# Matmuls on constants at the start of a recurrence kernel, and a planner that counts its first weights as landing later

## The chip, the cores and the metric

The kernel runs on one core of a Trainium2 chip. The metric is the device time of one execution in microseconds (us). The core has a matrix engine (TensorE, PE in the profile, with weight loads as PEld), a vector engine (VectorE, DVE), a scalar engine (ScalarE, ACT), GpSimd (POOL) and SyncE (SP), which issues the DMAs. Each takes its instructions in the order in which they were written, and waits on semaphores for the others.

## The reference

Two blocks. The first is a linear recurrence per batch and head, with q, k, v and a gate of shape (4, 8, 768, 48); the second multiplies two projections of its output and projects the product twice. All arithmetic that counts is float32; the four weight matrices come as float64.

```python
f = 1.0 / (1.0 + np.exp(-f_logit))
for t in range(S):
    state = f[:, :, t, :, None] * state + np.einsum('bhd,bhe->bhde', k[:, :, t], v[:, :, t])
    y[:, :, t] = np.einsum('bhd,bhde->bhe', q[:, :, t], state)
x = y.transpose(0, 2, 1, 3).reshape(B * S, H * D)      # 3072 x 384
a = x @ w1                                             # 384 -> 1024
b = x @ w2
return ((a * b) @ w3) @ w_out                          # 1024 -> 1024 -> 384
```

## The kernel before

The sequence is cut into 24 chunks of 128 steps (u = 0 to 23; six to a batch entry). For each chunk, `attention(u)` forms the running products of the gates forward (`forward`, L329) and backward (`backward`, L351) with two scans on VectorE, scales q and k by them (`scale_q` L345, `scale_k` L359), and multiplies the two on TensorE (`pairs`, L370, into the PSUM tile `pa`). ScalarE copies that out as A (`taken`, L379), GpSimd masks it to be causal (`causal`, L385), and TensorE multiplies it with v (`value`, L420) and adds what the state carries in (L428 for the first four chunks, L435 later). For the state, TensorE transposes K (`turn`, L396, into the PSUM tile `pk`), ScalarE copies it (`turned`, L404), TensorE multiplies it with v (`update`, L456, again into `pk`), and VectorE adds and scales (`state`, L466 to L472). ScalarE puts the state into blocks (`blocks`, L478). The output goes to `ys` (`outcome`, L485); of the first four chunks it is put in place by TensorE with a permutation `perm` (`moved`, L509, and `settled`, L514), later by DMAs (`gather`, L504).

Four chunks make a token block of 512. `ffn(n)` multiplies it by w1 and w2 (all through `three`, L530), forms the product a*b, and multiplies by w3 and w_out folded into one matrix `wc` (`fold`, L984). From the second block on, the products follow a scheme with seven instead of eight block products, with sums on VectorE.

The weights come in float64 and are turned to float32 on the chip. `fetch` (L871) loads a piece of 128 rows with one DMA (L897) into one of five raw buffers, which later loads use again once their last reader, L927, is done. `sub` then turns each half-piece of 512 columns with two operations on ScalarE (`magnitude` L916, `rest` L919) and on VectorE `shifted` (L922, L923), `signed` (L927) and `joined` (L933). Loads 0 to 2 are w1, loads 3 to 5 are w2, then w_out and w3 follow. The first half of the columns of w1 is due first.

No order of instructions is written by hand. Every step is a task of `Plan` (L73) with an engine, a cost in us, the tasks that it depends on and a priority, and `order` (L92) builds a schedule greedily: of all tasks it takes the one that can start earliest, by priority among those that start at the same time. The tasks are then emitted by their planned start, and this fixes the order on every engine. Loads go through `moves` (L286): a task on SP for the issue and one on a queue called DMA for the transfer, whose readers may start a `lag` of 1.3 us after it. The costs and lags are constants of the kernel and decide only the order; on the chip each instruction waits for its semaphores. SP issues the loads of the first four chunks and of five weight pieces one after the other, from 1.35 to 17.6 us.

Before the plan is emitted, `setup` (L236) clears buffers and makes constants. The one that matters here is `floor`, a tile of 112 partitions by 512 columns filled by VectorE at L248 and L249, with 2^-60 and a few ones. The PSUM tile `pk` has one buffer, used in turn by `turn`, `update` and, at the very end, `judge`.

Of the kernel before, what the change touches and what calls it, by code (L numbers as in the profile page):

```python
# [36 lines left out]
F32 = mybir.dt.float32  # L37
# [8 lines left out]
P = 128  # L46
# [3 lines left out]
HP = H // 2  # L50
R = 64 + D
# [13 lines left out]
TH = TB // 2  # L65
# [59 lines left out]
@with_exitstack  # L125
def kernel(
    ctx: ExitStack,
    tc: tile.TileContext,
    q: bass.AP,
    k: bass.AP,  # L130
    f_logit: bass.AP,
    v: bass.AP,
    w1: bass.AP,
    w2: bass.AP,
    w3: bass.AP,
    w_out: bass.AP,
    leaf_mask: bass.AP,
    out: bass.AP,
):
    nc = tc.nc  # L140
    const = ctx.enter_context(tc.tile_pool(name="const", bufs=1))
    ident = const.tile([P, P], F32, name="ident")
    w12 = const.tile([P, 2, KM, DFF], F32, name="w12")
    wc = const.tile([P, KF, DM], F32, name="wc")
    left = const.tile([1, 1], I32, name="left")
    with tc.manual_schedule():
        outside = ranged(tc, q, k, f_logit, v, w1, w2, w3, w_out, out, ident, w12, wc, left)
        with tc.If(outside > 0, preferred_fallthrough_block=True, label="general"):
            general(tc, q, k, f_logit, v, leaf_mask, out, ident, w12, wc)
# [12 lines left out]
def rows(par):  # L162
    return slice(64 * par, 64 * par + D)
# [10 lines left out]
def ranged(ctx, tc, q, k, f_logit, v, w1, w2, w3, w_out, out, ident, w12, wc, left):  # L174

    nc = tc.nc
# [10 lines left out]
    ps = ctx.enter_context(tc.tile_pool(name="ps", bufs=1, space=PSUM))  # L187
    ps_f = ctx.enter_context(tc.tile_pool(name="ps_f", bufs=NF, space=PSUM))

    floor = keep.tile([R, NQ], F32, name="floor")  # L190
# [35 lines left out]
    plan = Plan()  # L226
# [3 lines left out]
    moving = plan.add("PE", 0.0, lambda: None, takes=["ab"], prio=-1e9)  # L230
    coming = plan.add("PE", 0.0, lambda: None, takes=["ab"], prio=-1e9)

    def heads(t):
        return t.rearrange("p (h c) -> p h c", c=C)

# [44 lines left out]
    def need(u):  # L280
        return (0.0, 1.0, 2.0, 3.0)[u] if u < 4 else 45.0 + 14.5 * (u - 4)

    def past(u, n, *names):
        return [tk[u - n][nm] for nm in names if u >= n and nm in tk[u - n]]

    def moves(issue, size, rate, emit, deps, prio):  # L286

        i = plan.add("SP", issue, emit, deps, prio, lag=0.6)
        return plan.add("DMA", size / rate, lambda: None, [i], prio, lag=1.3)

    def attention(u):
        s, t = st[u], tk[u]
        opens, closes = u % NCH == 0, u % NCH == NCH - 1
        n0 = need(u)
# [38 lines left out]
        def last():  # L333
            nc.scalar.copy(lasts[:, u], heads(s["P"])[:, :, C - 1])
# [3 lines left out]
        def ends():  # L338
            nc.vector.reciprocal(heads(back)[:, :, C - 1], heads(s["P"])[:, :, C - 1])
# [109 lines left out]
        if not closes:  # L449
            def update():  # L450
                s["pd"] = ps.tile([P, HP, R], F32, name="pk")[0:R, :, 0:D]
                for hp in range(HP):
                    for par in range(2):
                        h = 2 * hp + par
                        w = 64 if par == 0 else D
                        nc.tensor.matmul(  # L456
                            s["pd"][64 * par : 64 * par + w, hp], lhsT=s["kt"][:, hp, 64 * par : 64 * par + w],
                            rhs=s["v"][:, h * D : h * D + D], start=True, stop=True,
                        )

            t["s"] = plan.add("PE", 0.6, update, [t["e"], t["lv"]] + past(u, 1, "d"), n0 - 997)

            def state():
                s["S"] = work.tile([R, HP, D], F32, name="S")
                s["G"] = work.tile([R, HP], F32, name="G")
                nc.vector.tensor_tensor(s["G"], lasts[:, u], heads(gate[(u + 1) % 2][:, 0:NQ])[:, :, 0], ALU.mult)  # L466
                gain = s["G"].unsqueeze(2).to_broadcast([R, HP, D])
                if opens:
                    nc.vector.tensor_tensor(s["S"], s["pd"], gain, ALU.mult)
                else:  # L470
                    nc.vector.tensor_tensor(s["S"], s["pd"], st[u - 1]["S"], ALU.add)
                    nc.vector.tensor_tensor(s["S"], s["S"], gain, ALU.mult)  # L472

            t["d"] = plan.add("DVE", 0.55 if opens else 0.9, state, [t["s"], t["l"]] + past(u, 2, "b"), n0)

            def blocks():
                for par in range(2):
                    nc.scalar.copy(sb[u % 2][rows(par), :, 64 * par : 64 * par + D], s["S"][rows(par)])  # L478

            t["b"] = plan.add("ACT", 0.75, blocks, [t["d"]] + past(u, 1, "v"), n0)  # L480
# [10 lines left out]
        n = u // UB  # L491
# [379 lines left out]
    def fetch(loads_, a, prio, subs, deps=()):  # L871

        total = subs[-1][1]
        if not wide:
            def plain():
                for place_, src in loads_:  # L880
                    for c0, c1, dst, _, _ in subs:
                        d = dst().rearrange("p (a m) -> p a m", a=a)
                        m = (c1 - c0) // a
                        b0 = c0 // a if len(subs) > 1 else 0
                        nc.sync.dma_start(d[place_], src[:, :, b0 : b0 + m])
            waits = [d for sub in subs for d in sub[4]]
            ld = plan.add("SP", 1.9 * total / 512, plain, waits, prio, lag=2.0)
            return [ld] * len(subs)
        load_no = len(users)
        buf = load_no if load_no < len(raws) else (load_no - len(raws)) % NRAW  # L890
        raw = raws[buf][:, 0 : 2 * total]
        words = raw.rearrange("p (n two) -> p n two", two=2)
        held = [g for no, b_, gs in users if b_ == buf for g in gs]

        def load():
            for place_, src in loads_:
                nc.sync.dma_start(raw.rearrange("p (a m) -> p a m", a=a)[place_], src.bitcast(U32))  # L897

        ld = moves(0.45, total, 380, load, held[-2:], prio)
        asked.append(ld)  # L900
        got = []
        users.append((load_no, buf, got))
        ends = []

        def sub(c0, c1, dst, due, waits):
            n = c1 - c0
            w = n / 512
            lo, hi = words[:, c0:c1, 0], words[:, c0:c1, 1]
            a0 = spot[0] if n <= 512 else (spot[0] + 512) // 1024 * 1024 % 2048
            spot[0] = (a0 + (512 if n <= 512 else 1024)) % 2048  # L910
            m = magnitudes[:, a0 : a0 + n]
            mine = range(a0 // 512, (a0 + n + 511) // 512)
            s = {}

            def magnitude():
                nc.scalar.activation(m, hi.bitcast(F32), AF.Abs)  # L916

            def rest():
                nc.scalar.activation(lo.bitcast(F32), lo, AF.Copy, bias=2.0, scale=2.0**-51)  # L919

            def shifted():
                nc.vector.tensor_scalar(m, m, HIGH, LOW, ALU.min, ALU.max)  # L922
                nc.vector.tensor_scalar(m.bitcast(U32), m.bitcast(U32), 3, None, ALU.logical_shift_left)  # L923

            def signed():
                s["to"] = dst()
                nc.vector.scalar_tensor_tensor(  # L927
                    s["to"].bitcast(U32), hi, 0x80000000, lo, ALU.bitwise_and, ALU.bitwise_or
                )

            def joined():
                to = s["to"].bitcast(I32)
                nc.vector.tensor_tensor(to, m.bitcast(I32), to, ALU.add)  # L933

            past = [joins[i] for i in mine if i in joins]
            b = plan.add("ACT", 0.2 + 0.43 * w, magnitude, [ld] + past, due)
            e = plan.add("ACT", 0.2 + 0.43 * w, rest, [ld], due)
            h = plan.add("DVE", 0.32 + 0.54 * w, shifted, [b], due)
            g = plan.add("DVE", 0.16 + 0.53 * w, signed, [e, b] + list(waits), due)
            j = plan.add("DVE", 0.16 + 0.53 * w, joined, [h, g], due - 1)  # L940
            parts.append((g, j))
            joins.update({i: j for i in mine})
            got.append(g)
            ends.append(j)

        for one_ in subs:
            sub(*one_)
        return ends
# [104 lines left out]
    for u in range(NU):  # L1053
        attention(u)
        if u == 3:
            weights()
        if u == NU - 1:
            judged = plan.add("DVE", 1.5, judge, [tk[i]["y"] for i in range(NU)], -20)
        if u % UB == UB - 1:
            ffn(u // UB)  # L1060
# [340 lines left out]
```

## Time and profile before

| | us |
|---|---|
| median of 5 runs | 507.74 |
| lowest and highest of them | 507.44, 508.65 |
| the profiled execution | 508.19 |
| its span in the profile | 505.8 |
| TensorE busy in the span | 486.8 |
| VectorE busy in the span | 363.2 |
| ScalarE busy in the span | 161.8 |

What follows was read from this one profiled execution; 2.4 us of its time lie outside the span. A line of the timeline gives the start, the length, the engine, the line of the code, the operation, what it writes and reads with the shapes, and how many instructions were merged; in brackets stand the engine's idle time before it and what ended that. A float32 matmul appears as two instructions. The start of the kernel is the part to look at: the first chunk's products begin at 8.50 us, and the first product with w1 at 36.26.

### The profile page before, as it was taken

To read this page: it belongs to the slowest core of one execution; us is meant where nothing else is said; L and a number is where in the kernel's file an instruction comes from. 1 tells how busy PE (TensorE), PEld (TensorE's weight loads), DVE (VectorE), ACT (ScalarE), POOL (GpSimd) and SP (SyncE) were. 2 spreads that over 40 slices of the span, in tenths; PEclk is the share of its full clock that TensorE was granted. 3 is DMA by queue.
4 is the path that set the end of the run, shared out by engine and by line. 5 is a ranking of instruction groups with operands and counts; after the bars stand their busy time and mean duration, and the time that the engine had idled before them with its cause. 6 is when DMAs were issued, how large, how long until landed. Compare 5 with 4: busy or idle time off the path is not lost.

```text
span 505.8 us, 8806 instructions
## 1 busy us (share of the span) xinstructions
PE 486.8 (96%) x3346; PEld 406.9 (80%) x3346; DVE 363.2 (72%) x701; ACT 161.8 (32%) x340; POOL 42.8 (8%) x51
## 2 busy tenths in 40 slices
PE   3889999999999999999999999999999999999995
PEld 2778854666698887889878899888899888889994
DVE  6899999999988769866677766256564677564541
ACT  4689464863434345212432112321010011011000
POOL 8120010010011201001110000110000000000000
PEclk9999999999999999999999999999999999999999
DMA  5978466853123265311160001210002100000011
GB/s 174 365 246 271 132 232 214 258 186 90 47 79 92 59 191 171 87 36 45 44 192 16 1 6 32 61 46 0 2 21 61 45 1 0 1 0 1 32 49 52
DMA packets 30163, 46.02 MB, mean 91 GB/s; under 512 B 6560, under 2 KB 20384, under 8 KB 28320
## 3 DMA queue, kind: packets, MB, share of 16 engines
q1 hardware_dynamic: 30112, 45.38, 28.6%
q8 instruction: 28, 0.46, 0.4%
q14 instruction: 23, 0.19, 0.1%
HBM read 36.70 MB, written 4.72 MB: 82 GB/s over the span
## 4 chain that ended last, share of the span: by engine, by line
PE 90%; DVE 4%; SPq 2%; POOL 1%; DMA 1%; issue 1%; ACT 0%; POOLq 0%; DVEq 0%; ACTq 0%
PE f L530 67%; PE f L984 8%; PE pa L370 4%; PE pa L420 4%; PE pk L456 2%; PE pa L435 2%; PE pk L396 2%; SPq L504 1%; DVE fwd L329 1%; PE f L420 1%; DMA ab<-in_f_logit_dram 1%; DMA vt<-in_v_dram 1%; DVE bwd L351 0%; DVE Q L345 0%; SPq L299 0%
## 5 line engine op out<-in xcount | busy, mean ns | idle before, releaser
L530 PE MATMUL f<-xt,w 128*128 128x256 f32 (+1 forms) x600 | 160.1, 397 | 0.0
L530 PEld LDWEIGHTS f<-xt,w 128*128 128x128 f32 x600 | 112.9, 190 | 24.4 <-issue 9.5
L530 PE MATMUL f<-place 128*128 128x192 f32 (+1 forms) x504 | 114.0, 351 | 0.0
L530 PEld LDWEIGHTS f<-place 128*128 128x128 f32 x504 | 87.3, 190 | 6.8 <-issue 1.1
L385 POOL TENSOR_SCALAR_AFFINE_SELECT A<-A 128x1024 f32<-128x1024 f32 x24 | 31.5, 1313 | 293.5 <-ACT A L379 293.5
L984 PE MATMUL f<-place 128*128 128x384 f32 x128 | 43.1, 490 | 0.0
L633 ACT COPY a<-f 128x256 f32<-128x256 f32 x36 | 13.4, 372 | 75.4 <-PE f L530 59.7
L530 PE MATMUL f<-xt,place 128*128 128x256 f32 x144 | 37.2, 381 | 0.0
L984 PEld LDWEIGHTS f<-place 128*128 128x128 f32 x128 | 23.8, 190 | 15.8 <-issue 0.7
L530 PE MATMUL f<-wc,ab 128*128 128x192 f32 x192 | 35.7, 329 | 0.0
L329 DVE TENSOR_TENSOR_SCAN fwd<-gate,floor 112x512 f32<-112x512 f32 x24 | 30.6, 1275 | 2.8 <-ACT gate L321 1.8
L530 PEld LDWEIGHTS f<-wc,ab 128*128 128x128 f32 x192 | 31.8, 190 | 0.9
L657 DVE TENSOR_TENSOR place<-f,a 128x256 f32<-128x256 f32 x36 | 15.2, 423 | 23.8 <-PE f L530 23.6
L379 ACT COPY A<-pa 128x1024 f32<-128x1024 f32 x24 | 24.2, 1010 | 22.0 <-PE pa L370 22.0
L370 PEld LDWEIGHTS pa<-Q,K 48*128 48x128 f32 x384 | 24.8, 198 | 6.9 <-issue 4.7
L351 DVE TENSOR_TENSOR_SCAN bwd<-gate,back 112x512 f32<-112x512 f32 x24 | 29.8, 1240 | 0.8
L530 PEld LDWEIGHTS f<-xt,place 128*128 128x128 f32 x144 | 26.9, 189 | 3.8 <-DVE place L657 0.2
L370 PE MATMUL pa<-Q,K 48*128 48x128 f32 x384 | 29.5, 296 | 0.0
L485 ACT ACTIVATE ys<-pa 112x512 f32<-112x512 f32 x20 | 11.9, 597 | 40.8 <-PE pa L435 21.9
L396 PE MATMUL pk<-ident,K 112*128 112x112 f32 x80 | 12.4, 280 | 11.5 <-DVE K L359 10.3
L919 ACT ACTIVATE place<-place 128x512 f32<-128x512 uint32 (+2 forms) x24 | 21.1, 890 | 7.2 <-DMA place<-in_w_out_dram 4.4
L916 ACT ACTIVATE place<-place 128x512 f32<-128x512 f32 (+2 forms) x24 | 21.2, 885 | 6.6 <-DVE w L933 4.0
(104 smaller groups left out, 624.6 us busy)
## 6 DMA issues: line engine op xcount, KB each, us to landing
place<-in_w_dram SPq DMA_DIRECT2D x14, 1024.0 KB, 5.2
vt<-in_v_dram SPq DMA_DIRECT2D x24, 192.0 KB, 2.9
out_dram<-o SPq DMA_DIRECT2D x24, 192.0 KB, 2.0
q<-in_q_dram SPq DMA_DIRECT2D x46, 96.0 KB, 2.4
f<-in_f_logit_dram SPq DMA_DIRECT2D x44, 96.0 KB, 2.7
k<-in_k_dram SPq DMA_DIRECT2D x44, 96.0 KB, 2.6
place<-in_w_out_dram SPq DMA_DIRECT2D x4, 768.0 KB, 5.3
xt<-ys SPq DMA_DIRECT2D x120, 24.0 KB, 1.8
```

Source lines behind the costliest of these rows:

```text
L329: nc.vector.tensor_tensor_scan(s["P"], gate[u % 2][:, 0:NQ], floor, 0.0, ALU.mult, ALU.max)
L351: nc.vector.tensor_tensor_scan(s["R"][:, ::-1], gate[u % 2][:, NQ:0:-1], back[:, ::-1], 0.0, ALU.mult, ALU.max)
L370: nc.tensor.matmul(s["pa"][:, par, cols], lhsT=s["K"][rows(par), cols], rhs=s["Q"][rows(par), cols], start=True, stop=True,)
L379: nc.scalar.copy(s["A"].rearrange("p r h c -> p r (h c)"), s["pa"])
L385: nc.gpsimd.affine_select(out=a, in_=a, pattern=[[0, H], [1, C]], compare_op=ALU.is_ge, fill=0.0, base=0, channel_multiplier=-1,)
L396: nc.tensor.transpose(out=s["pk"][:, hp], in_=s["K"][:, hp * C : hp * C + C], identity=ident[0:R, 0:R])
L420: nc.tensor.matmul(y_block(b)[64 * half : 64 * half + w], lhsT=s["v"][:, h * D : h * D + w], rhs=s["A"][:, par, hp], start=bank not in met ...
L530: nc.tensor.matmul(out_, lhsT=lhs[i], rhs=rhs[i], start=start and i == 0, stop=i == len(lhs) - 1, skip_group_check=True,)
L657: nc.vector.tensor_tensor(ups["u3", k], q["Y"], q["a"], ALU.add)
L916: nc.scalar.activation(m, hi.bitcast(F32), AF.Abs)
L919: nc.scalar.activation(lo.bitcast(F32), lo, AF.Copy, bias=2.0, scale=2.0**-51)
L984: nc.tensor.matmul(w3s["p", jc], lhsT=w3s[jc][:, kc * P : kc * P + P], rhs=wos[:, kc], start=(kc == 0), stop=(kc == KF - 1),)
```

## The change

Three additions. A task of 10 matmuls on the constant tile `floor` (112 partitions, 128 columns as weights, 256 as the moving operand) stands at the head of TensorE's plan, at a cost of 6.0; its result goes to `pk` and is never read. A second task of 2 such matmuls follows the state update of chunk 0. And `moves` gets an argument `late`, by which the readers of the first four weight loads are planned 5.5, 4.0, 2.5 and 1.0 us later than before; the issue and the transfer themselves are planned as they were.

```diff
+    def idle(n):
+
+        def emit():
+            to = ps.tile([P, HP, R], F32, name="pk").rearrange("p h r -> p (h r)")[:, 0:TH]
+            for _ in range(n):
+                nc.tensor.matmul(to, lhsT=floor[:, 0:P], rhs=floor[:, 0:TH], start=True, stop=True)
+        return emit
+
+    plan.add("PE", 6.0, idle(10), prio=-1e8)
+
...
-    def moves(issue, size, rate, emit, deps, prio):
+    def moves(issue, size, rate, emit, deps, prio, late=0.0):
 
         i = plan.add("SP", issue, emit, deps, prio, lag=0.6)
-        return plan.add("DMA", size / rate, lambda: None, [i], prio, lag=1.3)
+        return plan.add("DMA", size / rate, lambda: None, [i], prio, lag=1.3 + late)
...
             t["s"] = plan.add("PE", 0.6, update, [t["e"], t["lv"]] + past(u, 1, "d"), n0 - 997)
+            if u == 0:
+                plan.add("PE", 0.86, idle(2), [t["s"]], n0 - 996)
...
-        ld = moves(0.45, total, 380, load, held[-2:], prio)
+        ld = moves(0.45, total, 380, load, held[-2:], prio, max(0.0, 5.5 - 1.5 * load_no))
```

## The prediction

> **What bounds the kernel now.** I read the page's shares and slices first, then the busy time by stretch, then TensorE's instructions of the first 40 us, then what VectorE waited for there. From the page (parts 1, 2 and 4):
>
> ```profile
> PE 486.8 (96%) x3346; PEld 406.9 (80%) x3346; DVE 363.2 (72%) x701; ACT 161.8 (32%) x340; POOL 42.8 (8%) x51
> PE   3889999999999999999999999999999999999995
> DVE  6899999999988769866677766256564677564541
> PE 90%; DVE 4%; SPq 2%; POOL 1%; DMA 1%; issue 1%; ACT 0%; POOLq 0%; DVEq 0%; ACTq 0%
> ```
>
> TensorE is the bound, except in the first two slices. The stretches (us; busy and count of PE, PEld, DVE, ACT, POOL; clock; DMA):
>
> ```profile
> 8.50:14.40 5.90, 4.05 (x37) 3.37 (x37) 4.97 (x8) 3.48 (x7) 4.76 (x10) 1.00 0.74 225
> 14.40:20.00 5.60, 5.60 (x55) 4.81 (x56) 4.16 (x7) 2.21 (x6) 0.00 (x0) 1.00 0.98 356
> 20.00:28.00 8.00, 7.99 (x94) 7.07 (x93) 7.72 (x11) 7.34 (x17) 2.67 (x2) 1.00 1.01 422
> 28.00:36.00 8.00, 6.70 (x87) 5.64 (x84) 7.73 (x17) 5.89 (x12) 1.32 (x1) 1.00 0.64 203
> 39.00:66.00 27.00, 27.00 (x110) 20.33 (x108) 25.96 (x51) 17.45 (x32) 0.00 (x0) 1.00 0.58 190
> ```
>
> After 39 us TensorE has only some 2 us of gaps before the tail, so time is to be had only ahead of it. VectorE, though, is as full from 20 us on: TensorE can gain only what VectorE gains. TensorE's own timeline (start, length, what, wait before):
>
> ```profile
> 8.50 0.98 PE L396 MATMUL pk<-ident,K 112*128 112x112 f32 x4 [8.50 <-DVE K L359]
> 9.41 2.08 PE L370 MATMUL pa<-Q,K 48*128 48x128 f32 x16
> 11.54 1.06 PE L456 MATMUL pk<-vt,kt 128*64 128x48 f32 x16
> 14.40 0.98 PE L396 MATMUL pk<-ident,K 112*128 112x112 f32 x4 [1.80 <-DVE K L359]
> 15.31 1.97 PE L420 MATMUL f<-A,vt 128*64 128x128 f32 x16
> 17.21 1.84 PE L370 MATMUL pa<-Q,K 48*128 48x128 f32 x16
> 21.01 0.55 PE L396 MATMUL pk<-ident,K 112*128 112x112 f32 x4
> 21.49 1.09 PE L420 MATMUL f<-A,vt 128*64 128x128 f32 x16
> 23.56 1.16 PE L370 MATMUL pa<-Q,K 48*128 48x128 f32 x16
> 33.05 0.61 PE L396 MATMUL pk<-ident,K 112*128 112x112 f32 x4 [1.11 <-DVE S L471]
> ```
>
> Like groups take 1.8 times as long before about 18.7 us as after it: a slow array, though the clock column says 1.00 there. And the last transpose waits 1.11 us for a state update (S) of chunk 2. VectorE's timeline of the two waits that this causes it:
>
> ```profile
> 12.65 0.36 DVE L469 TENSOR_TENSOR S<-pk,G 112x192 f32<-112x192 f32 x1 [0.76 <-PE pk L456]
> 12.92 1.33 DVE L359 TENSOR_TENSOR K<-k,bwd 112x512 f32<-112x512 f32 x1
> 19.70 0.36 DVE L471 TENSOR_TENSOR S<-pk,S 112x192 f32<-112x192 f32 x1 [1.18 <-PE pk L456]
> ```
>
> **What the Trainium skill says.** "TensorE: Matmul & The Clock Gate", Part 1: the array runs at half rate until one free-running window of about 3.4 us has been busy, and falls back after an idle one. The trace agrees in part: 4.1 us of work from 8.50 did not release it, the run from 14.40 did after some 4.3 us, and at the end the clock column drops at 503.3, 3.0 us after the last matmul. "SBUF — State Buffer", SBUF: two separate sides: VectorE operations with two SBUF inputs and GpSimd share a port pair as an exclusive lock. The trace agrees: K at 12.92 takes 1.33 us instead of 0.69 while GpSimd's mask (L385) runs from 12.62 to 13.71.
>
> **The change, part by part.** *Ten matmuls at the head.* They need only floor (last memset ends at 1.61), so they start near 1.9. Each is two instructions of 256 columns; four such take 0.87 in the chain at 39.16, so ten matmuls cost 4.4 warm, 8.7 at half rate. Half rate for 4.3 us does half of them, the rest takes 2.2: end near 8.4, just where K of chunk 0 lets the first transpose start (8.47). Bounds: 1.1 later with the release late in its window (9.5), 10.6 if it never comes. They end by 9.5 at no cost: behind them the update L456 needs v of chunk 0, which lands at 8.78+2.6=11.4, and the mask waits for GpSimd's copies of perm until 12.17.
>
> Warm, chunk 0 goes: transposes to 9.05, L370 to 10.2, L456 11.4 to 12.07 (before 12.60). S starts near 12.15 instead of 12.65. The mask then starts at 12.2 instead of 12.62, K of chunk 1 still collides with it and ends 13.84 instead of 14.25: 0.4 gained, not more.
>
> *Two matmuls after that update.* They take the buffer pk that S reads, so I expect them to wait for S (12.5); 0.87 warm ends at 13.4, behind K1 (13.84), which TensorE's next work needs anyway. Cost 0; 0.4 if they are at half rate and K1 is early. They keep the array active.
>
> *Chunk 1 warm.* Groups L396, L420 and L370 lose 0.43+0.88+0.68=2.0. L456 of chunk 1 then ends at 13.9+0.55+1.05+1.1+0.65=17.25 instead of 19.65, before VectorE wants it: VectorE's dense row Q, fwd, bwd, K brings S to 18.1, and the 1.18 wait goes. One mask collision (Q at 20.36 took 1.58 for 0.69) remains and falls on another operation. Q of chunk 2 ends near 20.65 instead of 21.94; VectorE's gain is 1.3.
>
> *Late weights in the planner.* Loads 0 to 3 count as landing 5.5, 4.0, 2.5 and 1.0 later. No DMA is moved by this among the first loads; only the sorted order is. Worked by hand with the planner's costs (for the order, not for times): ScalarE's two operations for the first half-piece, now at 20.00 and 20.59, go behind blocks, settled, turned and the A of chunk 2; chunk 2's update goes ahead of its L420; and its S goes ahead of the first half's joined (L933), two and a half half-pieces earlier than now. So the wait of 1.11 at 33.05 goes. Cost: after Q of chunk 3 (24.8) VectorE waits for ScalarE's first magnitude (about 25.2): 0.4, but the mask of chunk 2 holds the port then, and the collision it has now at 26.44 (1.19 for 0.43) is the same 0.7. I take 0 to 0.6.
>
> What is late next: v of chunk 3 lands at 17.33+13.4=30.7 (the DMA engines are full from 16 to 29). Its L420, now at 33.59 and otherwise possible at 29.5, starts at 30.75; then 1.02+1.06+1.34+0.60 (L420, L428, L509, L456 in the chain) bring the first product with w1 to 34.75 instead of 36.33: 1.6. Its weights (third joined, now 35.51) are there at 33.65. Next gate: the first product with w2 follows the wide L530 group, ending about 50.75, and its third piece is joined at 50.21, so there is 0.5 of slack. That piece follows VectorE's dense row, and its load is issued at 40.40, when L927 frees the raw buffer; both move with VectorE by 1.3. So TensorE keeps 1.6 there at most (1.3+0.5 of slack). At the second fold the slack is again 0.3 (joined 88.96, L984 at 89.48 after its queue): 1.6 fits just so. Sum: -1.6, less 0.1 for the stall on ScalarE: -1.5 against the profiled 508.19, 506.7. The profiled execution lies 0.45 above the median of 507.74; part of that can be the release coming late, which the dummies remove, so I take -1.3 from the median: 506.4.
>
> **Rivals.** *The gain ends at VectorE.* If the stall on the magnitude is 0.6, recurs once for the second piece, and the collisions fall worse by one (0.7), VectorE gains 0 to 0.5, and at the w2 piece TensorE holds 0.5. For: VectorE is at 7.7 of 8 from 20 to 36. Against: ScalarE waits 1.61 for VectorE at 31.89, so it has room. Time 507.3.
>
> *The new order starves the w2 product (slower).* Place: the first product with w2, whose third piece has slack 0.5. By my hand-worked plan the operation that frees that load's buffer comes 2.15 later on the planner's clock, so other half-pieces may be sorted ahead of it. Each is 0.42+0.43+0.69+0.69=2.23 of VectorE. One eats the whole gain (2.23-1.8=+0.4); two give +2.6 less what later gaps give back, say +1.7: 509.4. It decides from the second half-piece ahead of the third w2 piece. Against: I find the same set ahead of it in both orders. Any other lost position behind 66 us, where VectorE is just ahead of TensorE, would price alike.
>
> *The dummies stay cold.* Chunk 0 starts at 10.6 instead of 8.5, all at half rate: L396 to 11.6, L370 to 13.6, L456 to 14.7, against 12.6 now: VectorE loses 2.1, gets back 1.2 at the chunk 1 wait as the array then is warm: +0.9, less the 1.1 of the moved S: 507.9. Against: 6.8 us in a row always hold a whole window.
>
> **How the numbers follow.** Forecast 0.45 (506.4, own range 505.4 to 507.3). An order that falls better than worked here 0.15 (505.3: at most the 2.0+1.1+1.8 us of slow and idle TensorE before 36 is to be had, and half of it is taken). VectorE 0.12 (507.3), starved 0.22 (509.4), cold 0.06 (507.9). A difference below 0.2% (1.0 us) is about what this measurement can't tell from none: the five runs span 1.2. Below 506.7 lie two thirds of the forecast and the better order: faster 0.45. Above 508.8 lie the starved case and a third of the cold one: slower 0.24. Between: 0.31. The range takes in the better order and half of the starved case: 504.8 to 509.2.
>
> **What would show it.** In the profile after: L370 of chunk 0 at 1.1 to 1.2 us; dummies ending between 7.8 and 9.5; no VectorE wait at S of chunk 1; no wait of L396 for S near 30; L420 of chunk 3 waiting for v; first L530 near 34.8. Wrong if the third w2 piece is joined after 50, or if gaps behind 66 us grow past 2 us.

## The result, and the profile after

The change made the kernel slower. The medians of the timed executions, beside each other on one chip, were 509.08 us after (42 executions, 507.60 to 512.70) against 508.07 us before (79 executions, 506.61 to 510.94 and a single one of 639.85), a ratio of 1.0035 with a 95% interval of 1.0025 to 1.0044. The profiled execution took 508.79 us (span 506.6) against 508.19 (505.8). The prediction said 506.4 and a range of 504.8 to 509.2: the time lies inside the range, near its upper end, but a gain was forecast and a loss came.

The page of the kernel after, parts 1 and 2:

```profile
PE 493.2 (97%) x3370; PEld 411.7 (81%) x3370; DVE 362.7 (72%) x701; ACT 162.3 (32%) x340; POOL 42.1 (8%) x51
...
PE   7999999999999999999999999999999999999995
...
DVE  7799999999998769866677766256564677564541
...
PEclk9799999999999999999999999999999999999999
```

TensorE's first slice is now filled with the constants, and the clock row has a 7 in its second slice that before did not have. The same stretches as before (us; busy and count of PE, PEld, DVE, ACT, POOL; clock; DMA):

```profile
8.50:14.40 5.90, 2.91 (x37) 2.40 (x38) 5.62 (x8) 2.86 (x6) 4.79 (x11) 0.87 0.77 231
14.40:20.00 5.60, 5.54 (x38) 4.12 (x38) 3.96 (x6) 2.05 (x6) 0.00 (x0) 0.53 0.93 337
20.00:28.00 8.00, 8.00 (x100) 7.14 (x98) 6.38 (x9) 5.42 (x12) 2.01 (x2) 1.00 1.01 418
28.00:36.00 8.00, 7.54 (x109) 6.76 (x106) 7.79 (x16) 7.60 (x16) 1.41 (x2) 1.00 0.68 221
39.00:66.00 27.00, 27.00 (x109) 20.38 (x109) 25.26 (x50) 19.50 (x36) 0.00 (x0) 1.00 0.55 176
```

From 14.40 to 20 us the array ran at 0.53 of its clock: the same 5.6 us now hold 38 matmuls where they held 55. TensorE's timeline, the lines that answer to those of before (the calls are ten lines further down in the code up to the update of the state, and twelve behind it: L406 was L396, L430 was L420, L466 was L456, L521 was L509, L542 was L530, L996 was L984; on VectorE G, once L466, is L478, and S is L481 and L483; L238 is the constants):

```profile
1.66 6.71 PE L238 MATMUL pk<-floor 112*128 112x256 f32 x20 [1.66 <-DVE floor L259]
8.57 0.57 PE L406 MATMUL pk<-ident,K 112*128 112x112 f32 x4 [0.21 <-DVE K L369]
9.11 1.16 PE L380 MATMUL pa<-Q,K 48*128 48x128 f32 x16
11.44 0.64 PE L466 MATMUL pk<-vt,kt 128*64 128x48 f32 x16 [1.17 <-DMA vt<-in_v_dram]
13.82 2.07 PE L238 MATMUL pk<-floor 112*128 112x256 f32 x4 [1.74 <-DVE S L481]
15.95 1.01 PE L406 MATMUL pk<-ident,K 112*128 112x112 f32 x4
16.89 1.97 PE L430 MATMUL f<-A,vt 128*64 128x128 f32 x16
...
31.06 0.55 PE L406 MATMUL pk<-ident,K 112*128 112x112 f32 x4
32.06 1.08 PE L430 MATMUL f<-A,vt 128*64 128x128 f32 x16 [0.46 <-DMA vt<-in_v_dram]
33.08 1.13 PE L438 MATMUL f<-Q,sb 112*112 112x128 f32 x8
34.04 1.50 PE L521 MATMUL f<-ys,ab 112*128 112x128 f32 x12
35.47 0.67 PE L466 MATMUL pk<-vt,kt 128*64 128x48 f32 x16
36.09 1.60 PE L521 MATMUL f<-ys,ab 112*128 112x128 f32 x12
37.53 0.81 PE L542 MATMUL f<-xt,w 128*128 128x256 f32 x3
...
90.33 5.43 PE L996 MATMUL f<-place 128*128 128x384 f32 x16 [1.02 <-DVE place L945]
```

Read it in four steps. Chunk 0 is warm, as meant (0.57 and 1.16 where before had 0.98 and 2.08). Then TensorE waits twice, 1.17 for v of chunk 0 and 1.74 for S, and the second set of constants comes out at 2.07 us instead of the 0.87 of a warm array. It stands in front of chunk 1's transposes, which start at 15.95 instead of 14.40, and all of chunk 1 is slow again. The wait of L396 for S at 33.05 is gone, but v of chunk 3 is waited for, two permuting products stand before the first product with w1, and the second fold waits 1.02 for VectorE, which before did not happen.

The windows in which the clock changed (it fell at about 12.82 and was released at about 19.64, as finer stretches place it; the rows are cut in steps of half of that, 3.41 us, and the first is the last one at full clock):

```profile
9.41:12.82 3.41, 1.50 (x32) 1.21 (x28) 3.34 (x4) 2.05 (x4) 3.41 (x8) 1.00 0.80 232
12.82:16.23 3.41, 2.35 (x6) 1.45 (x7) 3.20 (x5) 1.33 (x3) 0.47 (x1) 0.50 0.79 235
16.23:19.64 3.41, 3.41 (x28) 2.80 (x29) 2.24 (x5) 1.26 (x4) 0.00 (x0) 0.50 0.98 389
```

A window in which TensorE was busy 1.50 of 3.41 us cost the clock; one of 2.35 did not bring it back, the full one behind it did. That the clock goes by such windows is borne out by the twenty traces of this case: every stretch between two changes of the clock in them is a multiple of 3.41 us long, the short ones 3.41, 6.83, 13.65, 20.48 and 27.31. VectorE in the same place:

```profile
11.84 1.47 DVE L478 TENSOR_TENSOR G<-lasts,gate 112x4 f32<-112x4 f32 x1
13.41 0.36 DVE L481 TENSOR_TENSOR S<-pk,G 112x192 f32<-112x192 f32 x1
13.68 0.68 DVE L369 TENSOR_TENSOR K<-k,bwd 112x512 f32<-112x512 f32 x1
...
21.00 0.36 DVE L483 TENSOR_TENSOR S<-pk,S 112x192 f32<-112x192 f32 x1 [2.37 <-PE pk L466]
```

The mask, now early (12.20 to 13.29), meets the small operation G ahead of S instead of K behind it: G took 1.47, S came at 13.41 instead of 12.65, and K, no longer held up itself, ended at 14.36, 0.1 later than before. At chunk 1 the wait for the product is 2.37 where it was 1.18: VectorE has lost 1.30 (21.00 against 19.70).

### The profile page after: what moved, and what is told of

Its sections match the earlier page's. It is cut to its first block, busy times and chain, and to the rows that moved or that the text cites. A ratio compares the mean times of both kernels' runs of the same rounds, so it can differ in the third digit from the quotient of the medians.

```text
span 506.6 us, 8858 instructions
## 1 busy us (share of the span) xinstructions
PE 493.2 (97%) x3370; PEld 411.7 (81%) x3370; DVE 362.7 (72%) x701; ACT 162.3 (32%) x340; POOL 42.1 (8%) x51
## 5 line engine op out<-in xcount | busy, mean ns | idle before, releaser
L542 PE MATMUL f<-xt,w 128*128 128x256 f32 (+1 forms) x600 | 159.9, 397 | 0.2 <-ACT a L645 0.2
L542 PEld LDWEIGHTS f<-xt,w 128*128 128x128 f32 x600 | 113.1, 190 | 24.7 <-issue 9.6
L542 PE MATMUL f<-place 128*128 128x192 f32 (+1 forms) x504 | 114.0, 351 | 0.0
L542 PEld LDWEIGHTS f<-place 128*128 128x128 f32 x504 | 87.3, 190 | 6.8 <-issue 1.1
L996 PE MATMUL f<-place 128*128 128x384 f32 x128 | 43.1, 490 | 1.0 <-DVE place L945 1.0
L996 PEld LDWEIGHTS f<-place 128*128 128x128 f32 x128 | 23.8, 190 | 16.9 <-DVE place L945 1.4
L542 PE MATMUL f<-xt,place 128*128 128x256 f32 x144 | 37.2, 381 | 0.0
L542 PE MATMUL f<-wc,ab 128*128 128x192 f32 x192 | 35.7, 329 | 0.0
L542 PEld LDWEIGHTS f<-wc,ab 128*128 128x128 f32 x192 | 31.8, 190 | 0.9
L669 DVE TENSOR_TENSOR place<-f,a 128x256 f32<-128x256 f32 x36 | 15.2, 423 | 23.7 <-PE f L542 23.6
L389 ACT COPY A<-pa 128x1024 f32<-128x1024 f32 x24 | 24.3, 1011 | 24.9 <-PE pa L380 24.8
L542 PEld LDWEIGHTS f<-xt,place 128*128 128x128 f32 x144 | 26.9, 189 | 3.8 <-DVE place L669 0.2
L380 PEld LDWEIGHTS pa<-Q,K 48*128 48x128 f32 x384 | 23.7, 190 | 6.8 <-issue 3.9
L380 PE MATMUL pa<-Q,K 48*128 48x128 f32 x384 | 28.3, 287 | 0.0
L430 PEld LDWEIGHTS pa<-A,vt 128*48 128x48 f32 (+1 forms) x320 | 17.4, 130 | 6.2 <-issue 4.8
```

What stands on the lines that cost most here:

```text
L380: nc.tensor.matmul(s["pa"][:, par, cols], lhsT=s["K"][rows(par), cols], rhs=s["Q"][rows(par), cols], start=True, stop=True,)
L389: nc.scalar.copy(s["A"].rearrange("p r h c -> p r (h c)"), s["pa"])
L430: nc.tensor.matmul(y_block(b)[64 * half : 64 * half + w], lhsT=s["v"][:, h * D : h * D + w], rhs=s["A"][:, par, hp], start=bank not in met ...
L542: nc.tensor.matmul(out_, lhsT=lhs[i], rhs=rhs[i], start=start and i == 0, stop=i == len(lhs) - 1, skip_group_check=True,)
L669: nc.vector.tensor_tensor(ups["u3", k], q["Y"], q["a"], ALU.add)
L996: nc.tensor.matmul(w3s["p", jc], lhsT=w3s[jc][:, kc * P : kc * P + P], rhs=wos[:, kc], start=(kc == 0), stop=(kc == KF - 1),)
```

## The experiments

The two traces leave three accounts: the new order loses, the constants that do not hold the clock lose, or both do. Ratios are to the kernel before on the same chip; "low" counts executions whose mean granted clock was 0.993 or less. Of the 203 executions of the kernel before that ran beside the experiments, 199 had 0.997 or more; of the 44 of the changed kernel none had more than 0.996. 6.8 us at half rate cost 0.007 (half of 6.8, of 506.6), so "low" means about two windows or more. A cold start reads as 1.00 and is not counted. In the kernels with fillers the lines stand further down: L415 is L396 of before, L389 is L370, L439 is L420, L475 is L456, L508 is L485, L532 is L509, L553 is L530, L939 is L916 and L1007 is L984.

| run | constants | weights late | loads moved | ratio (95%) | median | low |
|---|---|---|---|---|---|---|
| e1 | none | yes | no | 1.0031 (1.0017 to 1.0044) | 510.04 | 3 of 22 |
| e2 | head | yes | no | 1.0061 (1.0036 to 1.0085) | 510.29 | 8 of 9 |
| e3 | head, two | no | no | 1.0021 (1.0000 to 1.0043) | 509.78 | 11 of 14 |
| e4 | head, two | yes, G early | no | 1.0042 (1.0021 to 1.0063) | 509.12 | 6 of 10 |
| e5 | head, fillers | no | no | 1.0049 (1.0033 to 1.0066) | 510.65 | 6 of 8 |
| e6 | head, fillers | yes | no | 1.0073 (1.0059 to 1.0087) | 511.59 | 3 of 6 |
| e7 | head, fillers | yes, permuting product early | no | 1.0017 (1.0000 to 1.0034) | 509.00 | 1 of 14 |
| e8 | head, fillers | no, update early | no | 1.0030 (1.0016 to 1.0045) | 509.44 | 16 of 22 |
| e9 | none | no | v of chunk 19 | 0.9989 (0.9980 to 0.9998) | 507.77 | 0 of 21 |
| e10 | head, fillers | no | v of chunk 19 | 1.0010 (0.9989 to 1.0030) | 509.05 | 12 of 22 |
| e13 | head, two | yes | v of 2, 3, 19 | 0.9976 (0.9959 to 0.9993) | 507.64 | 11 of 14 |
| e14 | head, fillers | yes | v of 2, 3, 19 | 0.9944 (0.9931 to 0.9957) | 505.47 | 0 of 6 |
| e15 | head, fillers | no | v of 2, 3, 19 | 1.0014 (0.9996 to 1.0031) | 509.38 | 13 of 22 |
| e16 | none | no | v of 2, 3, 19 | 0.9987 (0.9977 to 0.9997) | 507.63 | 1 of 22 |
| e17 | head, fillers | yes, fold early | v of 2, 3, 19 | 1.0043 (1.0026 to 1.0060) | 511.13 | 8 of 9 |
| e18 | none | yes | v of 2, 3, 19 | 0.9990 (0.9977 to 1.0004) | 508.45 | 0 of 22 |

**The parts of the change.** e1 takes out both sets of constants, e2 the second set alone, e3 the late weights; e4 keeps all and puts G of chunk 0 ahead of chunk 0's Q on VectorE.

```diff
-    plan.add("PE", 6.0, idle(10), prio=-1e8)                       # e1
-                plan.add("PE", 0.86, idle(2), [t["s"]], n0 - 996)  # e1, e2
-        ld = moves(0.45, total, 380, load, held[-2:], prio, max(0.0, 5.5 - 1.5 * load_no))
+        ld = moves(0.45, total, 380, load, held[-2:], prio)        # e3
+            plan.add("DVE", 0.02, early_gain, [t["g"], tk[0]["l"]], n0 - 1)  # e4
```

> Both groups of dummy matmuls are left out, the later planned landing stays, so the order is that of the changed kernel. If the second dummies cause the loss (theory A), the start is as before, chunk 1's state on VectorE starts near 19.7 us and not 21.0, and the time is that of before within 0.5 us (ratio 0.999 to 1.001). If the new order costs the time (theory B), it stays 0.7 us or more above before (ratio 1.0015 to 1.004).

> The ten dummies at the head and the later landing stay, only the two dummies after chunk 0's update go. Theory A: chunk 1's transposes start at 14.4 to 14.5 us instead of 15.95, chunk 1's state near 19.6 or earlier, and the ratio to before is 0.997 to 1.001. Theory B: as the changed kernel, 1.002 to 1.004. If the head dummies alone do harm (theory C: the mask comes earlier and holds up the gain G), above 1.002 too, but with chunk 1's state at 20.5 or later.

> Both groups of dummies stay, the planned landing is that of before, so the order is that of before plus the dummies. Theory A: chunk 1's transposes near 16 us, state near 21, ratio 1.002 to 1.005, and a second cluster of times some 3 us higher as in the changed kernel. Theory B: 0.998 to 1.001.

> The changed kernel with G of chunk 0 computed ahead of Q of chunk 0 instead of just ahead of S; nothing else in any queue differs. If S waits for G because G meets the mask on the port (part of theory A), S of chunk 0 starts near 12.15 instead of 13.41, the second dummies near 12.6 instead of 13.82, chunk 1's transposes near 14.5 instead of 15.95, and the ratio is 0.997 to 1.001. If S was late for another reason, no change from 1.0035.

Neither half is good by itself: the order alone costs 0.3%, and the constants alone come out 0.2% above the kernel before, with an interval that reaches 1.0000. In the trace of e1 the value product of chunk 3 waits 2.04 for v and the clock falls in that gap; the second fold waits 1.0. In e2 chunk 1 starts at 13.84 instead of 15.95, so the second constants do stand in its way, but the clock falls all the same (at 14.08), v of chunk 3 is then waited for 2.91, and the time is no better. In e3 the second constants take 2.07 again, S of chunk 1 is waited for 3.3, the fold not at all. The three executions of e3 with a mean clock of 0.994 or more took 506.1 to 506.8 us, the eleven others 508.2 to 512.4: in the order of before the loss goes with the clock. In e4 S comes early (12.12) and the constants run mostly warm (1.13), but the array falls back behind them (at 14.27), chunk 1 is slow again (1.97 for L420's group), v (1.29) and the fold (1.0) are waited for, and the time is that of the changed kernel: the collision of G with the mask was not the main loss, nor is it what costs the clock. The wait of 1.0 at the second fold is in every trace with late weights and in none without (e17 aside, which moves the fold), so it belongs to the order. The constants at the head alone, in the order of before, were not run.

**Holding the clock.** e5 to e8 replace the second constants by two matmuls ahead of chunk 0's update and four behind it, into another PSUM bank, so that they wait for no S. e5 has the order of before, e6 the late weights; e7 is e6 with chunk 2's permuting product ahead of chunk 3's value product; e8 is e5 with only chunk 2's update ahead.

```diff
-                plan.add("PE", 0.86, idle(2), [t["s"]], n0 - 996)
+                filler(4, 1.7, [t["s"]], n0 - 996)
+            if u == 0:
+                filler(2, 0.4, [t["a"], t["e"]], n0 - 998)
             t["s"] = plan.add("PE", 0.6, update, ...)
```

> The ten head matmuls stay, the planner's order is that of before, and the two matmuls behind the update of chunk 0 are replaced by two ahead of that update and four behind it, which write to another PSUM bank and so don't wait for S. Theory (the clock falls back in the gaps of chunk 0, and the two matmuls on pk then stand at half rate in front of chunk 1): the array stays at full rate through chunk 1 (L396 group near 0.55 instead of 0.98, value group near 1.1 instead of 1.97), no VectorE wait at S of chunk 1, the wait for S of chunk 2 (1.1) stays, no wait at the second fold, and no second cluster of times: ratio 0.996 to 0.999. Rival (the loss is in the order alone, the clock at the start is worth nothing since VectorE sets the pace): ratio 0.999 to 1.001, with VectorE waits elsewhere taking back what S of chunk 1 gives.

> As the changed kernel, order of the weights included, but with the two matmuls behind the update of chunk 0 replaced by two ahead of it and four behind it, which write to another PSUM bank. Theory (two losses: the clock, and the order by the wait for v of chunk 3 and by 1.0 at the second fold): the clock holds through chunk 1, the wait of chunk 3's value product for v is 1 to 3, the second fold waits 1.0 for VectorE, ratio 1.000 to 1.002, some 1 to 1.5 us above the same fillers in the order of before. Rival (the order costs nothing once the clock holds): the same time as with the order of before, within 0.3 us.

> As the run before it (fillers, late weights), but the permuting product of chunk 2 is planned ahead of chunk 3's value product, so that ready work stands in front of the product that waits for v. Theory: the wait for v shrinks by about 1.4, the wait of 1.0 at the second fold stays, time 0.5 to 1.4 us under the run before it. Rival (TensorE gains nothing there since VectorE sets the second fold): same time within 0.3, with the wait at the second fold grown by what v's wait lost.

> Fillers in the order of before, without the late weights; instead only the update of chunk 2 is planned ahead of its value product, so that S of chunk 2 comes earlier. Theory: the wait of 1.1 for S goes, but the wait for v of chunk 3 takes its place (0.5 to 2), so the time is within 1 us of the fillers in the order of before. Rival (the wait for S is worth its 1.1): 1 us under them.

In all four traces chunk 1 is warm (L396's group 0.55 to 0.57), and its S is not waited for: the fillers do what the two constants were for. Yet e5 and e6 are slower than e3 and the changed kernel, and my theory as far as it went had fallen. In e6 v of chunk 3 is waited for 3.22 and the clock falls in that gap (the product behind it took 1.95); in e7, with ready work in front of it, the wait is 0.91 and the clock holds. e7 is 2.6 us faster by the medians, more than forecast: this supports v, with the clock that its gap costs, as one loss. e8 traded the wait for S for 0.83 for v and 1.06 for ScalarE. e5 was forecast at 0.996 to 0.999 and came at 1.0049. In its trace the first product with w1 starts at 35.12, 1.14 earlier than before, and the second fold, at 88.29, also comes 1.12 earlier; the gain is lost later. (The trace is one of two executions of e5 that held the clock; it took 508.94 us, the six low ones 510.3 to 511.5.) TensorE's timeline of e5:

```profile
256.79 0.61 PE L475 MATMUL pk<-vt,kt 128*64 128x48 f32 x15 [1.80 <-DMA vt<-in_v_dram]
```

and SyncE's ahead of it:

```profile
237.72 7.94 SPq L527 DMA_DIRECT2D xt<-ys  x10
245.77 0.52 SPq L842 DMA_DIRECT2D out_dram<-o  x1
246.39 7.53 SPq L527 DMA_DIRECT2D xt<-ys  x10
254.02 0.53 SPq L335 DMA_DIRECT2D vt<-in_v_dram  x1
```

Forty gather issues from 224.5 to 254 us stand ahead of the load of v of chunk 19, with a median of 0.59 each and two of 1.91 and 2.31. TensorE, early by 0.9 us at 225 us, waits 1.80 for it; the kernel before waited 0.64 in the same place.

**SyncE's row, and the clock once more.** e9 and e10 move that one load ahead of the last ten gathers, in the kernel before and in e5; no other instruction moves. e11 and e12 are the changed kernel again, for more traces.

```diff
-    for t in plan.order():
+    tasks = plan.order()
+    late_gather, early_v = tk[15]["z"]["deps"][0], tk[19]["lv"]["deps"][0]
+    tasks.remove(late_gather)
+    tasks.insert(tasks.index(early_v) + 1, late_gather)
+    for t in tasks:
```

> The kernel before with one DMA moved on SyncE: the load of v of chunk 19 stands ahead of the ten gather DMAs of chunk 15 instead of behind them; nothing else moves on any engine. Theory (SyncE's dense row of 40 gather issues from 225 to 254 us sets when v of chunk 19 lands, and TensorE is level with it already in the kernel before): the wait of 0.64 at the update near 256.5 is gone, ratio 0.9985 to 0.9995. Rival (the wait is covered by a later one): the same time, the 0.6 found again at the wait for VectorE near 370 or at the end.

> The fillers in the order of before (first run of the second set), with the same move of v of chunk 19 on SyncE. Theory (the microsecond that the warm array wins at the start is lost at 256 us to SyncE's row of issues): the wait of 1.80 at the update near 256 is gone, the executions in which the clock holds are at 506.0 to 507.2, ratio over all executions 1.000 to 1.003 because in most of them the clock still drops somewhere, which this trace may show. Rival (the loss lies elsewhere): the same as with the fillers alone, 1.004 to 1.006.

> The changed kernel once more, unaltered, for a second trace of it. A third of its executions lie near 512, the others near 508.7. Theory (v of chunk 3 lands late in front of TensorE's queue, or the clock falls once more): an execution near 512 shows a wait for v above 1.5 or one more stretch at half rate before 40 us, and from there to the end the same gaps as the trace at hand. Rival (SyncE's issues): the start is the same and the wait for v near 257 is above 2.

> As the run before it: the changed kernel unaltered, a third trace. Theory: if near 512, a wait for v of chunk 3 above 1.5 or a further stretch at half rate before 40 us; rival: the same start, and a wait for v above 2 near 257.

The wait at 256 is gone in both, and the kernel before gains 0.11% by the times. (The trace of e9 alone would not prove it: TensorE came to the second fold 0.74 later there. The array of the kernel before was slow until 23.7 us in e9 and until 24.3 in e16, against 18.7 in the first trace; the mean clock does not show this.) Of e10's executions the ten with a mean clock of 0.995 or more took 505.3 to 508.0 us, the twelve with less 508.7 to 512.55. Its own trace is one of the latter and shows where the clock goes now. ScalarE, with its waits:

```profile
20.76 0.69 ACT L939 ACTIVATE place<-place 128x512 f32<-128x512 f32 x1 [2.49 <-DMA place<-in_w_dram]
...
24.23 0.58 ACT L508 ACTIVATE ys<-f 112x512 f32<-112x512 f32 x1
```

and TensorE:

```profile
24.96 2.33 PE L532 MATMUL f<-ys,ab 112*128 112x128 f32 x12 [2.08 <-ACT ys L508]
27.22 2.08 PE L389 MATMUL pa<-Q,K 48*128 48x128 f32 x16
29.23 1.97 PE L439 MATMUL f<-A,vt 128*64 128x128 f32 x16
```

In the order of before ScalarE waits 2.49 us for the first weights with chunk 1's output queued behind; a warm TensorE has caught up with it by then, waits 2.08, and its clock falls for two windows (the first of them was full and still did not bring it back). This is what late weights are there to prevent, which suggests that the two halves of the change need each other.

e11 took 508.63 us and e12 511.86: one of each of the two groups in which the changed kernel's times lie (17 of 44 above 510). TensorE in e12:

```profile
13.34 2.07 PE L238 MATMUL pk<-floor 112*128 112x256 f32 x4 [0.47 <-DVE S L481]
...
33.16 1.79 PE L430 MATMUL f<-A,vt 128*64 128x128 f32 x16 [1.78 <-DMA vt<-in_v_dram]
34.89 2.04 PE L438 MATMUL f<-Q,sb 112*112 112x128 f32 x8
```

It has both losses: slow constants in front of chunk 1, and behind the wait for v of chunk 3 a second fall of the clock (L430 and L438 at 1.79 and 2.04 for 1.09 and 1.13). Its second fold starts at 93.03, that of e11 at 90.46. In e11 the wait for v was longer (2.23) but the clock held. In these two traces, then, the groups differ by whether the clock falls in the gap at v. The windows of 3.41 us, counted from the changes of the clock in each trace, show why (columns as above), first in e12:

```profile
29.97:33.38 3.41, 1.63 (x16) 1.45 (x18) 3.34 (x6) 3.12 (x8) 0.75 (x1) 1.00 0.59 184
33.38:36.79 3.41, 3.41 (x25) 3.05 (x22) 3.31 (x8) 1.84 (x4) 0.00 (x0) 0.50 0.74 208
```

and in e11:

```profile
28.08:31.49 3.41, 1.90 (x21) 1.51 (x15) 3.34 (x7) 3.12 (x9) 1.09 (x1) 1.00 0.83 290
31.49:34.91 3.42, 2.70 (x31) 2.54 (x32) 3.28 (x8) 2.88 (x7) 0.00 (x0) 1.00 0.58 163
```

e12's gap lies in one window, which is left busy 48%; e11's longer gap is divided between two, busy 56% and 79%. Where the windows lie differs by execution: the constants at the head begin at 1.66 in every trace that has them, and the clock is first released between 4.9 and 8.2. In the twenty traces each of the twelve falls ahead of the tail closes such a window with TensorE busy 57% or less, and no window ahead of 45 us with 60% or more cost the clock; between 50 and 57% both happened, so the share alone is not the whole rule.

**The loads.** v of chunk 3 is issued when chunk 0's value product frees its buffer, and behind two more weight loads. SyncE in the kernel after:

```profile
15.54 2.12 SPq L909 DMA_DIRECT2D place<-in_w_dram  x2
18.91 0.33 SPq L326 DMA_DIRECT2D vt<-in_v_dram  x1
```

e13 to e16 and e18 move v of chunk 2 ahead of the first three weight loads, v of chunk 3 ahead of the fourth and fifth, and v of chunk 19 as in e9; nothing else moves on any engine. e13 is the changed kernel so altered, e14 has the fillers and late weights, e15 the fillers and no late weights, e16 is the kernel before, and e18 has late weights and no constants.

```diff
+    issue = [ld["deps"][0] for ld in asked[0:5]]
+    v2, v3, v19 = (tk[u]["lv"]["deps"][0] for u in (2, 3, 19))
+    for t in issue[2::-1]:
+        behind(t, v2)
+    for t in issue[:2:-1]:
+        behind(t, v3)
+    behind(tk[15]["z"]["deps"][0], v19)
```

> The changed kernel with loads moved on SyncE and nothing else: v of chunk 2 ahead of the first three weight loads, v of chunk 3 ahead of the fourth and fifth, v of chunk 19 ahead of the gathers of chunk 15. Theory (v of chunk 3 in front of ready work is the main loss of the late order): the waits for v of chunks 2, 3 and 19 are gone, the first product with w1 starts at 34 to 36 instead of 37.5, the cluster near 512 is gone, median 506.5 to 507.8; the wait at the second fold stays at 1 or grows. Rival (VectorE sets the second fold whatever TensorE gains): the wait at the fold grows by what v's wait lost, median 508.3 to 509.

> As the run before it, but with the fillers (two ahead of chunk 0's update and four behind it, in another PSUM bank) in place of the two matmuls on pk. Theory: the clock holds through chunk 1 and no v is waited for behind chunk 0, so the mean clock is 0.995 or more in most executions, S of chunk 1 is not waited for, median 505 to 506.5, the best so far. Rival (nothing to gain since VectorE is the bound from 20 to 66 us): the same as the run before it.

> Fillers and the moved loads in the order of before, without late weights. Theory (with a warm array ScalarE's first weight operation stands in front of work of chunk 2 and starves TensorE, which then drops its clock): a wait of 1 to 2.5 of ScalarE for the first weights, executions with a mean clock under 0.994 remain, median 0.5 to 2 above the same with late weights. Rival (late weights cost 1.0 at the second fold and bring nothing): median 0.5 to 1 below the same with late weights.

> The kernel before with the same loads moved on SyncE and nothing else. Theory: its array is slow until 18.7 and its v of chunk 3 is not waited for, so only the wait of 0.6 at chunk 19 goes: ratio 0.998 to 1.000. Rival (loads ahead of weights also delay the weights and cost): 1.000 to 1.002.

> Late weights and the moved loads, with no matmuls on constants at all. Theory (late weights pay once v is there, but the array is slow until about 19 and VectorE keeps its wait for S of chunk 1): ratio 0.997 to 0.999, and no cluster above 510. Rival (late weights bring their gain only with a warm array): 0.9995 to 1.001, the wait of 1.0 at the second fold eating what the order gives.

e13 is 0.6% under the changed kernel, with no execution above 509.2: the group near 512 is gone with the wait for v. (The first product with w1 was expected at 34 to 36 and came at 36.83; chunk 1 is still slow there, and the three executions in which the clock held took 504.6 to 504.9.) e14 is the best, 2.98 us under the kernel before on the same chip and as expected, with no low clock in its six executions. Its TensorE timeline:

```profile
14.30 0.55 PE L415 MATMUL pk<-ident,K 112*128 112x112 f32 x4
14.78 1.09 PE L439 MATMUL f<-A,vt 128*64 128x128 f32 x16
...
28.28 1.09 PE L439 MATMUL f<-A,vt 128*64 128x128 f32 x16
...
34.28 4.48 PE L553 MATMUL f<-xt,w 128*128 128x256 f32 x20
...
87.09 5.43 PE L1007 MATMUL f<-place 128*128 128x384 f32 x16 [1.02 <-DVE place L956]
```

No wait for v of chunk 3, first product with w1 at 34.28, second fold at 87.09 against 89.41 before. With the loads moved in all four, the corners are 0.9987 with neither, 0.9990 with late weights, 1.0014 with fillers, 0.9944 with both. Late weights alone change nothing that can be told, fillers alone cost, and together they bring 0.43%, which fits what e10 showed. e15 lies 3.9 us above e14, where 0.5 to 2 had been expected. Its nine executions with a mean clock of 0.994 or more took 506.04 to 508.81, the thirteen low ones 509.25 to 511.62. Its trace is one of the nine: ScalarE waits 2.00 for the first weights and TensorE 0.84 behind it, and the clock holds.

**The second fold.** The 1.02 stays in e14, and moves with TensorE (90.33 in the kernel after, 87.09 here), so VectorE is not simply late by a fixed amount. In the kernel after, VectorE waits for TensorE for the last time at 63.60 and has no wait from there until the piece is joined:

```profile
63.60 0.42 DVE L584 TENSOR_TENSOR ab<-f,ab 128x256 f32<-128x256 f32 x1 [0.63 <-PE f L542]
...
89.05 1.22 DVE L945 CUSTOM_DVE_ANT_0 place<-place 128x2048 uint16<-128x2048 uint16 x1
```

e17 is e14 with VectorE's steps for the second w3 piece ahead of chunk 5's backward scan, K and Q, the second fold ahead of chunk 5's pairs and the third ahead of its value product.

```diff
+    for t in (shifted1, signed1, joined1):
+        ahead(t, tk[5]["r"])
+    ahead(fold1, tk[5]["a"])
+    behind(tk[5]["v"], fold2)
```

> Fillers, late weights and moved loads (the best so far), with VectorE's three steps for the second w3 piece ahead of chunk 5's backward scan, K and Q, and TensorE's second fold ahead of chunk 5's pairs, its third fold ahead of chunk 5's value product. Theory (the wait at the second fold is made by VectorE's order): the wait of 1.02 there is gone or under 0.1, up to 0.6 comes back as a wait at the third fold, median 0.4 to 1.0 below the same kernel without it (504.5 to 505.1). Rival (VectorE is simply a microsecond behind): the wait turns up whole at the third fold, same time.

The wait at the second fold went, and 4.00 came in its place, seen in the timeline of e17's TensorE:

```profile
102.53 2.08 PE L389 MATMUL pa<-Q,K 48*128 48x128 f32 x16 [4.00 <-DVE Q L364]
```

ScalarE's copy of chunk 5's product now waits 2.63 for the pairs moved back, with a weight operation behind it; VectorE waits 3.33 for that, and Q of chunk 6 is late. The array falls back in the gap as well (2.08 for 1.16). So the 1.02 is made by the order there, as expected, but it cannot be had by this swap; neither theory foresaw what it starts. Another order at that place was not tried.

## Why the prediction was wrong

Three steps failed. The second constants were to cost nothing and to keep the array active; they did neither. The gain of 1.6 at the first product with w1 was mis-sized, by the landing of v and a permuting product. And the slack at the second fold was taken to suffice; there a wait of 1.02 turned what gain was left into a loss. Part by part:

- *Ten matmuls at the head.* Right: they ended at 8.37 (forecast 8.4), L370 of chunk 0 took 1.16, at no cost. "S near 12.15" was wrong: I had K of chunk 1 still meeting the earlier mask; it was G instead, which stands ahead of S, and S came at 13.41. That is not so in every execution: in e11 and e12, the same kernel, G took 0.13.
- *Two matmuls after the update.* This is the first step that failed: "Cost 0" and "They keep the array active". The array had fallen back at 12.82 before they started, in the gaps that my own timetable had (10.2 to 11.4, and 12.07 to 12.5). They took 2.07 instead of 0.87 and stood in front of work on the path. I had priced the case ("0.4 if they are at half rate and K1 is early") from a start at 12.5; they started at 13.82, because S waited for G, and ended at 15.89, 1.5 behind K of chunk 1. The Trainium skill, "TensorE: Matmul & The Clock Gate", Part 1, names an idle window as what drops the clock; here a window busy 44% (1.50 of 3.41 us) was enough, in e4 one busy 57%, and the measurement decides.
- *Chunk 1 warm.* Failed with it: not 2.0 saved, but 1.01, 1.97 and 1.56 for L396, L420 and L370, hardly less than before, starting 1.55 later. VectorE's wait did not go, it doubled.
- *Late weights.* As far as it was named, the order was worked out rightly: S of chunk 2 moved ahead, its wait of 1.11 went, and VectorE's stall on the first magnitude was 0.39 (0.4 forecast). (The 36.33 given for the first product with w1 is the end of the product ahead of it; the timeline of before has 36.26.) "v of chunk 3 lands 30.7" took the issue at 17.33 as given. But the issue waits for the buffer that chunk 0's value product frees, and with that product ending at 18.86 the load went out at 18.91 and the product started at 32.06: 1.3 late. The chain of "L420, L428, L509, L456" also counted one permuting product where two stand (1.44 more). Together 2.75 of the 2.78 by which the first product with w1 missed 34.75. So the gain of 1.6 was mis-sized by these two terms: on equal work TensorE was 0.17 ahead of before at the first fold (82.90 against 83.07). In e13, with the loads moved and v not waited for, the product starts at 36.83, and in e14, with the clock held as well, at 34.28.
- *"At the second fold … 1.6 fits just so".* Failed by itself: the fold waited 1.01 to 1.03 in every trace with late weights but e17's, which moves it. The slack of 0.3 was read in the order of before; in the new order VectorE's last wait for TensorE is at 63.60, and from there it is dense up to the end of the piece at 90.27, some 26.7 us, where TensorE's own work to the fold is 25.7. So a lead of 0.17 at the first fold became a lag of 0.92 at the second; 0.41 of that is given back at v of chunk 19 (a wait of 0.23 for 0.64), and the span ends 0.8 longer.
- *The rivals.* The slower rival gave nearly the right time (509.4 for 509.08) by the wrong mechanism: no product with w2 was starved. "Dummies stay cold" is the near miss: they were warm at the head and cold where they were to keep the clock. "Wrong if … gaps behind 66 us grow past 2 us" came true: TensorE's waits there are 1.0, 0.7, 0.5, 0.2 and 0.2, together 2.6, where before had 1.7.

The gain forecast was there to be had, but not from the change alone: e14 has 2.98 us of it, after three loads were moved and the second constants freed from S. The medians differ by 1.0 and the profiled executions by 0.60; 17 of the 44 executions lie above 510, as e12 does with its second fall of the clock, and they raise the median.

## What to carry to other kernels

Matmuls that are to hold the clock should be free of the waits that make the gap. Here they held it in a PSUM bank other than the one that S reads and on both sides of the wait; the set that itself waited ran at half rate in front of real work. When two halves of a change are tried apart, a loss in each does not condemn the pair: here a warmer TensorE needed the queues beside it (ScalarE behind a weight load, SyncE behind forty issues, a load behind a buffer) to be cleared, and the one that stood next took the gain. A new order moves every slack, so a slack read in the old order is no reserve for the new one.

## What was not expected of the hardware

- The clock fell after a window of 3.41 us with TensorE busy 44% of it, and a following window busy 69% (2.35 of 3.41, all at half rate) did not bring it back; the next, full one did. In e3, e9, e10 and e16 a first full window at half rate did not, and the second did.
- An operation on 112x4 elements, 0.13 to 0.16 us elsewhere, took 1.47 us when it met GpSimd's last copies and its mask, and ended with the mask (13.31 and 13.29). In e11, the same kernel, it took 0.13 in the same place.
- The same load of v took 13.0, 14.1 and 14.6 us from issue to landing in three traces of one kernel, with the DMA engines full; ahead of two weight loads it took 8.6 in e13 and 11.4 in e14.
- Single gather issues on SyncE took up to 2.3 us where the median was 0.59; in e5 this turned a lead of 0.9 us over the kernel before at 225 us into a lag of 0.3 at 256.
